# A first round of 432 rows for 448 in a three-layer kernel, and four instructions of the capacity at another place

## The chip, the core and the metric

The kernel runs on one core of one Trainium2 chip. The metric is the device time of one execution in microseconds (us). The core's engines run their own queues in order: TensorE (PE; PEld is its weight load), VectorE (DVE), ScalarE (ACT), GpSimd (POOL) and SyncE (SP, which issues most DMAs). Matmuls and extractions go through PSUM banks, everything else through SBUF.

## The reference

Three layers, one behind the other: a recurrent attention over 4 x 8 heads of 768 steps, a mixture of 8 experts with one expert a token, and a dense layer. Cut to the part that the change touches:

```
def _moe_ref(x, w_gate, w1, w2, capacity):
    logits = x @ w_gate                      # 3072 tokens, 320 numbers, 8 experts
    expert_idx = np.argmax(logits, axis=1)
    gate_w = softmax(logits)[arange(N), expert_idx]
    for i in range(N):                       # rows of an expert, in the order of tokens
        e = expert_idx[i]
        if counts[e] < capacity:             # capacity = N // E * 2 = 768
            disp[e, counts[e]] = x[i]; pos[i] = counts[e]; counts[e] += 1; keep[i] = True
    h = np.maximum(einsum('ecd,edf->ecf', disp, w1), 0.0)     # 320 -> 1024
    y = einsum('ecf,efd->ecd', h, w2)                         # 1024 -> 320
    out[i] = gate_w[i] * y[expert_idx[i], pos[i]] if keep[i] else 0

def _moe2_ref(x, w_in, w_out):               # 320 -> 2048 -> 320
    h = x @ w_in
    return np.where(h > 0, h, np.exp(np.minimum(h, 0)) - 1) @ w_out
```

All inputs are random; the router therefore spreads the 3072 tokens over the experts unevenly around 384.

## The kernel before

**Stages.** `attention` works through 24 units of 128 tokens, in an order that is written out by hand in the table `ORDER` (a word a step; `steps` maps the first letters to functions). `ffn` follows with the experts and the dense layer. While attention runs, TensorE, VectorE, ScalarE and GpSimd share its small steps; its last steps put the last units' rows in place.

**Rows of an expert.** `x_out` makes a unit's rows with their logits; `route` and `route_mm` give each row its number within its expert; `scatter` writes the rows with an indirect DMA from GpSimd (L567) into `disp`, a DRAM tensor in which expert e has ES rows and its first row is at e*ES + SL. The experts' *first round* takes SL rows of every expert as four tiles of SL/4. Rows behind a shorter expert's last are zero (`zero_d`). Expert 0's rows are read back by `first_rows` (step `F`, function `first`); the rows of the last two units don't make that trip, but are placed by a one-hot matmul (`hot`, L587 and L588 build it on VectorE).

**The expert stage.** `experts(0)` runs eight `Turned` blocks. A block's rows, transposed, stand in PSUM (`pt`); `prep` makes a high part XH (ScalarE, L953) and a low part XL (VectorE, L954: the transposed rows less XH). A block has eight steps f. `s1` of a step multiplies the weights with the rows: 8 matmuls with SL columns (L969: four with XH, two with XL, two with XS, which holds both parts of the last 64 numbers). ScalarE makes H (L1099), VectorE L (L1100), and three steps later `s2` multiplies H and L with the second weights: 8 matmuls with SL columns (L1034 to L1044). Four PSUM banks are shared by `s1` and the transposes. The next expert's rows come by DMA (L1086), are scaled by their gate (VectorE L1073 to L1079, ScalarE L1093) and are transposed on TensorE (L934) between the steps.

**Weights.** A half of an expert's weights (128 x 2816 numbers, 1408 KB) is fetched by SyncE into one of two buffers (L802, L804). `split` then makes a high part on ScalarE (L776, four a half) and a low part on GpSimd (L781, sixteen a half). A fetch waits until the split of the half two before it has read its buffer.

**Counts and the capacity.** `marks`, at the head of the expert stage, turns the 64-bit capacity into a float with four small VectorE instructions (L1262 to L1265) and sets constants on GpSimd (among them `one`, L1268). `counts`, during the first expert's steps, sums the experts' rows and derives the places of the outputs and the number of rounds: it is one if no expert has more rows than SL (or the capacity). `overflow` holds a loop for the later rounds; it makes the experts and the dense layer again.

**The dense layer.** Six blocks of 512 tokens take the experts' outputs in expert order from `xt` (L1303, L1304) and scatter the result to its tokens (L1314).

The lines at the head of the expert stage:

```
second = split(1)
go(second, 5)                     # half 1: four L776, sixteen L781
if not dyn:
    marks()                       # L1262 to L1275
bl[0].start(None if dyn else turned)      # L953, L954
fetch(2)
```

Of the kernel before, what the change touches and what calls it, by code (L numbers as in the profile page):

```python
# [20 lines left out]
D = 320  # L21
NTOK = 3072
SL = 448
ES = 8 * SL
# [51 lines left out]
def attention(tc, nc, e_in, v_tok, d_in, wg, disp, xt, cst, ring, early, early_w, cv, cap, after):  # L76
# [499 lines left out]
    def hot(u):  # L576

        xo, w = st["XO", u], slice(0, D + 1)
        if u < NU - 1:
# [8 lines left out]
        nc.vector.tensor_tensor(oh.rearrange("p (i r) -> p i r", i=4), cst["row"].unsqueeze(1).to_broadcast([128, 4, 112]),  # L588
                                p.unsqueeze(2).to_broadcast([128, 4, 112]), op=ALU.is_equal)
# [7 lines left out]
    def first():  # L597
        nc.gpsimd.iota(cst["row"], pattern=[[1, 112]], base=SL, channel_multiplier=0, allow_small_or_imprecise_dtypes=True)
        nc.gpsimd.iota(cst["off"], pattern=[[-112, 4]], base=0, channel_multiplier=0, allow_small_or_imprecise_dtypes=True)
        first_rows(nc, cst, disp)  # L600

    def zero_d(e):
        nc.sync.dma_start(out=disp[e * ES + SL:e * ES + 2 * SL, :].rearrange("(p i) d -> p (i d)", p=112).rearrange("p (x d) -> p x d", d=188),
                          in_=zr[0:112, 0:188].unsqueeze(1).to_broadcast([112, 7, 188]))

    def zero_x():
        nc.sync.dma_start(out=xt[D:D + 1, :].rearrange("o (p d) -> (o p) d", p=16), in_=zr[0:16])
# [58 lines left out]
    for i in range(4):  # L666
        for k, c in enumerate(cols):
            nc.tensor.matmul(turned[k][0:c.stop - c.start, 112 * i:112 * i + 112], X[0:112, i, c], ident[0:112, 0:112], start=False, stop=False)
# [7 lines left out]
def first_rows(nc, cst, disp):  # L676
    dv = disp.rearrange("(e r i p) d -> e r p i d", e=8, i=4, p=112)
    X = cst["x"][:, 0:4 * RW].rearrange("p (i d) -> p i d", i=4)
    for i in range(4):
        nc.sync.dma_start(out=X[0:112, i], in_=dv[0, 1][:, i])  # L680


def consts(p):
# [15 lines left out]
    c["row"] = c["x"][:, 1536 + RW:1648 + RW]  # L699
# [187 lines left out]
def ffn(tc, nc, cst, disp, xt, w1, w2, w32, out, ring, W0, cv, ps, turned):  # L887
# [19 lines left out]
    class Block:  # L907
# [91 lines left out]
        def out(s):  # L999
            s.Y = ap.tile([128, 1344], F32, tag="Y", name="Y")[:, 0:1280].rearrange("p (i d) -> p i d", i=4)  # L1000
# [16 lines left out]
    class Turned(Block):  # L1017
# [50 lines left out]
    def soft(s, tag="s", lg=None):  # L1068

        t = lambda nm, sh: ap.tile(sh, F32, tag=tag + nm, name=nm, bufs=1)[0:112]  # L1070
        g, x = t("g", [128, 4]), t("x", [128, 4, 8])
        lg = s.X[0:112, :, D + 1:RW] if lg is None else lg
        nc.vector.tensor_reduce(g, lg, axis=AX.X, op=ALU.max)  # L1073
        nc.vector.tensor_tensor(x, lg, g.unsqueeze(2).to_broadcast([112, 4, 8]), op=ALU.subtract)
# [7 lines left out]
    def rows(src, gate=True):  # L1082

        def load(s, now):
            s.X = s.XF[:, 0:4 * RW].rearrange("p (i d) -> p i d", i=4)
            nc.sync.dma_start(out=s.X[0:112], in_=src)  # L1086
# [5 lines left out]
            for i in range(4):  # L1092
                nc.scalar.mul(s.X[0:112, i, 0:D], s.X[0:112, i, 0:D], g[:, i:i + 1])  # L1093
# [22 lines left out]
    def gates():  # L1116
# [26 lines left out]
        nc.vector.scalar_tensor_tensor(out=t, in0=t, scalar=over["cap"], in1=OH, op0=ALU.is_lt, op1=ALU.mult)  # L1143
# [10 lines left out]
        nc.vector.scalar_tensor_tensor(out=epos, in0=eb, scalar=1.0 / 8, in1=pos, op0=ALU.mult, op1=ALU.add)  # L1154
# [30 lines left out]
    dv = disp.rearrange("(e r i p) d -> e r p i d", e=8, i=4, p=112)  # L1185
# [5 lines left out]
    def experts(r, dyn=False, more=None):  # L1191
# [4 lines left out]
        for e in range(8):  # L1196
            if dyn:
                src = dv[e, bass.ds(r, 1)].rearrange("r p i d -> (r p) i d")
                dst = yr[SL * e:SL * e + SL, :].rearrange("(i p) d -> p i d", p=112)

                def store(Y, i, dst=dst):
                    if i == 3:
                        nc.sync.dma_start(out=dst, in_=Y[0:112])
                bl.append(Block(Ws[e], rows(src), relu, store, P=112))
            else:
# [5 lines left out]
                bl.append(Turned(Ws[e], rows(dv[e, 1], e > 0), relu, store, P=112))  # L1211
# [47 lines left out]
    def marks():  # L1259

        cw, cf = cst["cap"], ap.tile([128, 4], F32, name="cf", bufs=1)
        nc.vector.tensor_copy(cf[:, 0:2], cw)  # L1262
        nc.vector.tensor_scalar(cf[:, 2:3], cf[:, 0:1], 0.0, 4294967296.0, op0=ALU.is_lt, op1=ALU.mult)
        nc.vector.scalar_tensor_tensor(out=cf[:, 3:4], in0=cf[:, 1:2], scalar=4294967296.0, in1=cf[:, 2:3], op0=ALU.mult, op1=ALU.add)
        nc.vector.tensor_tensor(cf[:, 3:4], cf[:, 3:4], cf[:, 0:1], op=ALU.add)  # L1265
        over["cap"] = cf[:, 3:4]
# [3 lines left out]
        for i in range(4):  # L1270
            nc.gpsimd.iota(start[:, i:i + 1], pattern=[[0, 1]], base=112 * i, channel_multiplier=1, allow_small_or_imprecise_dtypes=True)
# [5 lines left out]
    def late_gate(B):  # L1277

        yield
        lg = ap.tile([128, 4, 8], F32, name="lgx", bufs=1)[0:112]  # L1280
# [9 lines left out]
        for i in range(4):  # L1290
            nc.tensor.matmul(p[:, 112 * i:112 * i + 112], g[:, i:i + 1].to_broadcast([112, 128]), ident[0:112, 0:112], start=True, stop=True)
# [66 lines left out]
    def counts():  # L1358
# [14 lines left out]
        nc.vector.tensor_scalar(rn[:, 1:2], rn[:, 0:1], float(SL // 8), None, op0=ALU.add)  # L1373
        nc.vector.tensor_scalar(rn[:, 2:3], over["cap"], float(SL), None, op0=ALU.min)
# [8 lines left out]
        over["n"] = nc.values_load(ri[0:1, 0:1], min_val=1, max_val=8)  # L1383
# [122 lines left out]
```

## Time and profile before

| | us |
|---|---|
| three timed runs | 1041.87, 1044.39, 1047.43 (median 1044.39) |
| the profiled execution | 1040.54 |
| its span, first to last instruction | 1038.7 |
| TensorE busy | 950.6 (92%) |
| VectorE, GpSimd, ScalarE busy | 738.3, 617.1, 516.6 |
| mean granted TensorE clock | 0.952 |

The profiled execution is one run, 3.85 us under the median of the others. A busy time is a sum over the whole span; what a stage is bound by is read from that stage alone. Matmuls overlap in the records: one with 448 columns is shown with 0.36 us, but the next begins 0.20 us later, so that their pace is read from their starts. Starts are in us from the span's start.

### The profile page before, as it was taken

What the parts mean: (1) busy time and instruction counts of PE and PEld (TensorE: products, weight loads), DVE (VectorE), ACT (ScalarE), POOL (GpSimd) and SP (SyncE); (2) the same over time, 40 slices, a digit from 0 to 9 for tenths busy, and PEclk for the clock granted to TensorE, in tenths of its full rate; (3) what the DMA queues carried; (4) which work ended last, traced back from release to release, by engine and by line L of the source; (5) the groups of instructions that cost most, each with busy time, mean ns of one, the idle gap of its engine ahead of it and who ended that gap; (6) DMA issues with size and microseconds to landing.
All of it is one profiled execution on the core that took longest, in us unless ns stands there. A gap on an engine that the chain in (4) does not pass through costs nothing.

```text
span 1038.7 us, 25351 instructions
## 1 busy us (share of the span) xinstructions
PE 950.6 (92%) x9994; PEld 860.9 (83%) x9994; DVE 738.3 (71%) x1291; ACT 516.6 (50%) x1013; POOL 617.1 (59%) x929
## 2 busy tenths in 40 slices
PE   4758989989899999789999999999999999999993
PEld 4758878888789888678889888888899888899993
DVE  8846848788675687658778877576766777677760
ACT  3636635666454434245544555565555555554550
POOL 4766979489898833467768787953333333333332
PEclk9967889999899999989999999999999999999997
DMA  6758875666565774646776866501010000100000
GB/s 161 174 159 173 182 162 120 144 139 145 127 120 119 171 195 99 170 141 203 214 236 201 250 186 217 187 23 26 27 27 26 11 28 13 27 26 1 26 2 28
DMA packets 181448, 121.69 MB, mean 117 GB/s; under 512 B 106256, under 2 KB 167336, under 8 KB 179688
## 3 DMA queue, kind: packets, MB, share of 16 engines
q1 hardware_dynamic: 175652, 99.63, 38.0%
q10 hardware_dynamic: 2500, 9.21, 3.4%
q0 software_dynamic: 3168, 11.14, 3.0%
q8 instruction: 81, 1.33, 0.5%
q14 instruction: 47, 0.39, 0.1%
HBM read 86.89 MB, written 33.05 MB: 115 GB/s over the span
## 4 chain that ended last, share of the span: by engine, by line
PE 54%; DVE 17%; DMA 16%; issue 5%; ACT 3%; POOL 3%; SPq 0%; ACTq 0%; DVEq 0%; POOLq 0%
PE ph L969 20%; DMA ring<-in_e_in_dram 5%; PE po L995 5%; PE po L996 5%; PE po L997 5%; DMA w<-E 4%; PE q L482 2%; PE sc L234 2%; DVE L L1100 1%; DVE ring L200 1%; PE x L519 1%; DVE E L860 1%; PE ut L426 1%; PE y L509 1%; DMA dab<-AB 1%
## 5 line engine op out<-in xcount | busy, mean ns | idle before, releaser
L781 POOL TENSOR_TENSOR ring<-ring,ring 128x64 fp32r<-128x64 f32 (+2 forms) x320 | 204.7, 675 | 72.4 <-ACT ring L776 72.4
L1114 POOL TENSOR_TENSOR L<-E,H 128x512 fp32r<-128x512 f32 x66 | 91.6, 1388 | 169.2 <-ACT H L1113 152.5
L969 PE MATMUL ph<-XH,ring 128*128 128x512 f32 (+1 forms) x640 | 169.9, 387 | 0.8 <-ACT XH L953 0.8
L1107 ACT ACTIVATE E<-N 128x512 f32<-128x512 f32 x96 | 60.7, 632 | 152.8 <-DVE N L1106 78.9
L310 POOL TENSOR_TENSOR X<-X,ring 128x60 f32<-128x60 f32 (+19 forms) x170 | 120.4, 708 | 13.3
L969 PEld LDWEIGHTS ph<-XH,ring 128*128 128x128 f32 x640 | 115.7, 190 | 14.9 <-ACT XH L953 1.4
L997 PE MATMUL po<-ring,L 128*128 128x320 f32 x384 | 119.4, 311 | 1.6 <-POOL L L1114 1.6
L995 PE MATMUL po<-ring,H 128*128 128x320 f32 x384 | 119.4, 311 | 0.2 <-ACT H L1113 0.2
L996 PE MATMUL po<-ring,H 128*128 128x320 f32 x384 | 119.2, 310 | 0.0
L969 PE MATMUL ph<-XL,ring 128*128 128x512 f32 (+1 forms) x320 | 97.9, 387 | 7.5 <-DVE XL L954 7.5
L969 PE MATMUL ph<-XS,ring 128*128 128x512 f32 (+1 forms) x320 | 96.9, 384 | 0.0
L1111 DVE SCALAR_TENSOR_TENSOR M<-E,M 128x512 f32<-128x512 f32 x96 | 78.0, 812 | 16.1 <-ACT M L1108 16.1
L1106 DVE TENSOR_SCALAR N<-ph 128x512 f32<-128x512 f32 x96 | 65.8, 685 | 27.7 <-PE ph L969 27.4
L308 POOL TENSOR_TENSOR ring<-X,ring 128x60 f32<-128x60 f32 (+19 forms) x108 | 65.0, 602 | 34.4 <-DMA ring<-dab 26.3
L995 PEld LDWEIGHTS po<-ring,H 128*128 128x128 f32 x384 | 72.8, 190 | 5.2 <-ACT H L1113 0.5
L996 PEld LDWEIGHTS po<-ring,H 128*128 128x128 f32 x384 | 72.7, 189 | 4.0
L969 PEld LDWEIGHTS ph<-XL,ring 128*128 128x128 f32 x320 | 60.7, 190 | 18.4 <-DVE XL L954 8.2
L997 PEld LDWEIGHTS po<-ring,L 128*128 128x128 f32 x384 | 72.7, 189 | 2.1 <-POOL L L1114 2.1
L1112 DVE SCALAR_TENSOR_TENSOR E<-ph,M 128x512 f32<-128x512 f32 x96 | 66.4, 692 | 8.1 <-DVE M L1111 0.5
L969 PEld LDWEIGHTS ph<-XS,ring 128*128 128x128 f32 x320 | 60.3, 189 | 11.2 <-DVE XS L954 0.4
L1100 DVE SCALAR_TENSOR_TENSOR L<-ph,H 128x448 fp32r<-128x448 f32 x64 | 39.4, 616 | 41.3 <-ACT H L1099 41.2
L1113 ACT CAST H<-E 128x512 fp32r<-128x512 f32 x96 | 59.0, 614 | 13.5 <-DVE E L1112 10.4
(261 smaller groups left out, 2176.5 us busy)
## 6 DMA issues: line engine op xcount, KB each, us to landing
ring<-in_w_dram SPq DMA_DIRECT2D x16, 640.0 KB
ring<-in_w_dram SPq DMA_DIRECT2D x32, 256.0 KB
dab<-AB SPq DMA_DIRECT2D x24, 256.0 KB
ring<-in_e_in_dram ACTq DMA_DIRECT2D x18, 321.6 KB
ring<-w SPq DMA_DIRECT2D x4, 1408.0 KB
disp<-ring SPq DMA_DIRECT2D x8, 575.8 KB
S<-in_w_out_dram SPq DMA_DIRECT2D x13, 320.0 KB
ring<-in_w_dram SPq DMA_DIRECT2D x32, 128.0 KB
```

The lines of the kernel that those rows point to most:

```text
L308: nc.gpsimd.tensor_tensor(tv, X[:, 0:n, s:s + 1].to_broadcast([128, n, m]), N[:, s:s + 1, s + 1:e].to_broadcast([128, n, m]), op=ALU.mult)
L310: nc.gpsimd.tensor_tensor(X[:, 0:n, s + 1:e], X[:, 0:n, s + 1:e], tv, op=ALU.subtract)
L781: s.nc.gpsimd.tensor_tensor(B[:, to], r[:, q], B[:, q].bitcast(F32), op=ALU.subtract)
L969: nc.tensor.matmul(p, l, r[:, 0:s.T], start=i == 0, stop=i == len(seq) - 1)
L995: nc.tensor.matmul(o, H[:, c], hb, start=f == 0, stop=False)
L996: nc.tensor.matmul(o, H[:, c], lb, start=False, stop=False)
L997: nc.tensor.matmul(o, L[:, c], hb, start=False, stop=f == s.W.nf - 1)
L1106: nc.vector.tensor_scalar(N, p, 0.0, None, op0=ALU.min)
L1107: nc.scalar.activation(out=E, in_=N, func=AF.Exp)
L1111: nc.vector.scalar_tensor_tensor(out=M, in0=E, scalar=1.0, in1=M, op0=ALU.add, op1=ALU.mult)
L1112: nc.vector.scalar_tensor_tensor(out=E, in0=p, scalar=0.0, in1=M, op0=ALU.max, op1=ALU.add)
L1114: eng.tensor_tensor(L, E, H.bitcast(F32), op=ALU.subtract)
```

## The change

SL becomes 432, SR = SL // 4 = 108 is the height of a tile, and ES becomes 9 SL, so that nine rounds of 432 rows hold what eight of 448 did. What was written for 112 rows and for a factor of 8 is written with SR and ES / SL. The four instructions of the capacity move from `marks` to `first`, and their tile `cf` from a pool of the feed-forward part to the constants. Cut to its core:

```
-SL = 448
-ES = 8 * SL
+SL = 432
+SR = SL // 4
+ES = 9 * SL
@@ hot
-oh "p (i r)": cst["row"] ... [128, 4, 112], p ... [128, 4, 112], op=ALU.is_equal
+oh "p (i r)": cst["row"] ... [128, 4, SR], p ... [128, 4, SR], op=ALU.is_equal
@@ first (step F)
+        cw, cf = cst["cap"], cst["cf"]
+        nc.vector.tensor_copy(cf[:, 0:2], cw)
+        nc.vector.tensor_scalar(cf[:, 2:3], cf[:, 0:1], 0.0, 4294967296.0, op0=ALU.is_lt, op1=ALU.mult)
+        nc.vector.scalar_tensor_tensor(out=cf[:, 3:4], in0=cf[:, 1:2], scalar=4294967296.0, in1=cf[:, 2:3], op0=ALU.mult, op1=ALU.add)
+        nc.vector.tensor_tensor(cf[:, 3:4], cf[:, 3:4], cf[:, 0:1], op=ALU.add)
-        nc.gpsimd.iota(cst["row"], pattern=[[1, 112]], base=SL, ...)
-        nc.gpsimd.iota(cst["off"], pattern=[[-112, 4]], base=0, ...)
+        nc.gpsimd.iota(cst["row"], pattern=[[1, SR]], base=SL, ...)
+        nc.gpsimd.iota(cst["off"], pattern=[[-SR, 4]], base=0, ...)
         first_rows(nc, cst, disp)
@@ consts
-    c["cap"] = p.tile([128, 2], I32, name="CAP")
+    c["cap"], c["cf"] = p.tile([128, 2], I32, name="CAP"), p.tile([128, 4], F32, name="CF")
@@ marks
-        cw, cf = cst["cap"], ap.tile([128, 4], F32, name="cf", bufs=1)
-        nc.vector.tensor_copy(cf[:, 0:2], cw)
-        ... the other three
-        over["cap"] = cf[:, 3:4]
         one = over["one"] = ap.tile([128, 8], F32, name="one", bufs=1)
@@ experts
-                bl.append(Turned(Ws[e], rows(dv[e, 1], e > 0), relu, store, P=112))
+                bl.append(Turned(Ws[e], rows(dv[e, 1], e > 0), relu, store, P=SR))
@@ counts
-        nc.vector.tensor_scalar(rn[:, 1:2], rn[:, 0:1], float(SL // 8), None, op0=ALU.add)
+        nc.vector.tensor_scalar(rn[:, 1:2], rn[:, 0:1], ES / SL, float(SL), op0=ALU.mult, op1=ALU.add)
-        nc.vector.tensor_scalar(rg, cst["ebase"], 1.0 / 8, rn[:, 1:2], op0=ALU.mult, op1=ALU.is_lt)
+        nc.vector.tensor_scalar(rg, cst["ebase"], 1.0, rn[:, 1:2], op0=ALU.mult, op1=ALU.is_lt)
-        over["n"] = nc.values_load(ri[0:1, 0:1], min_val=1, max_val=8)
+        over["n"] = nc.values_load(ri[0:1, 0:1], min_val=1, max_val=9)
```

In the loop of later rounds the division by 8 becomes one by 9, which takes one more instruction; the run shown doesn't enter that loop.

The order of instructions differs on VectorE alone; on the other engines the same instructions stand in the same order with smaller shapes. VectorE at the head of the expert stage, before (the one-hot of the last unit, the capacity, the low parts of the first expert's rows, two steps' L, and the second expert's row scaling):

```order
L588 TENSOR_TENSOR hot<-X_73,pos 128x448
L1262 CAST cf<-CAP 128x2
L1263 TENSOR_SCALAR cf<-cf 128x1
L1264 SCALAR_TENSOR_TENSOR cf<-cf 128x1
L1265 TENSOR_TENSOR cf<-cf 128x1
L954 TENSOR_TENSOR XL<-pt,XH 128x448 x2
L954 TENSOR_TENSOR XS<-pt,XS 64x448
L1100 SCALAR_TENSOR_TENSOR L<-ph,H 128x448 x2
```

The same place after the change:

```order
L589 TENSOR_TENSOR hot<-X_74,pos 128x432
L960 TENSOR_TENSOR XL<-pt,XH 128x432 x2
L960 TENSOR_TENSOR XS<-pt,XS 64x432
L1106 SCALAR_TENSOR_TENSOR L<-ph,H 128x432 x2
L1079 TENSOR_REDUCE g<-X_74 108x4
L1080 TENSOR_TENSOR x<-X_74,g 108x32
L1365 COPY cnt<-pc 128x8
L1367 SCALAR_TENSOR_TENSOR cs<-one,cnt 128x8
L1368 CAST bi<-cs 128x8
```

The low parts follow the one-hot with nothing between them; the scan and the CAST of the counts stand behind the second expert's logits as before. VectorE some 11 us earlier, at the step `F` after the change (the routing of unit 22, then the mask multiplication of the last unit's scores, which its y matmul reads); before, L547 was followed by L487 at once:

```order
L545 TENSOR_TENSOR roh<-req,rm_6292 128x8
L548 TENSOR_TENSOR ACC<-ACC,roh 128x8
L600 CAST CF<-CAP 128x2
L601 TENSOR_SCALAR CF<-CF 128x1
L602 SCALAR_TENSOR_TENSOR CF<-CF 128x1
L603 TENSOR_TENSOR CF<-CF 128x1
L488 TENSOR_TENSOR Qs<-q,mask 128x512 x2
```

The four stand there between the routing and the mask multiplication.

## Rows read from the trace of the kernel before

**Rows 1.** Stages: start:end and length, busy us (instructions) of five engines, clock, DMA.

```profile
437.40:665.50 228.10, 217.46 (x1094) 194.25 (x1095) 174.79 (x314) 116.11 (x215) 176.47 (x281) 0.98 0.66 201
665.50:1017.00 351.50, 349.69 (x1912) 312.97 (x1911) 246.18 (x352) 182.09 (x321) 131.33 (x137) 1.00 0.08 25
```

**Rows 2.** Timeline, expert stage's head: start, length, engine, line, tiles, count, [idle before].

```profile
436.72 8.28 POOL L781 TENSOR_TENSOR ring<-ring,ring 128x64 fp32r<-128x64 f32 x16
436.83 0.97 ACT L953 CAST XH<-pt 128x448 fp32r<-128x448 f32 x2 [2.56 <-PE pt L593]
436.85 8.24 DVE L1262 CAST cf<-CAP 128x2 f32<-128x2 int32 x1 [2.60 <-DMA ring<-in_w_dram]
437.41 1.30 PE L969 MATMUL ph<-XH,ring 128*128 128x448 f32 x4 [0.75 <-ACT XH L953]
...
445.58 1.15 DVE L954 TENSOR_TENSOR XL<-pt,XH 128x448 fp32r<-128x448 f32 x2
446.25 1.27 PE L969 MATMUL ph<-XL,ring 128*128 128x448 f32 x2 [7.54 <-DVE XL L954]
446.76 0.62 DVE L954 TENSOR_TENSOR XS<-pt,XS 64x448 fp32r<-64x448 f32 x1
...
450.87 1.06 PE L969 MATMUL ph<-XH,ring 128*128 128x448 f32 x4
```

**Rows 3.** One microsecond of that hole, columns as in rows 1.

```profile
440.00:441.00 1.00, 0.00 (x0) 0.00 (x0) 1.00 (x1) 0.00 (x0) 1.00 (x3) 0.50 0.24 32
```

**Rows 4.** Timeline of TensorE: one step with 448 columns, then the output stage.

```profile
655.86 0.96 PE L969 MATMUL ph<-XH,ring 128*128 128x448 f32 x4
...
659.06 0.96 PE L969 MATMUL ph<-XH,ring 128*128 128x448 f32 x4
...
759.82 0.30 PE L995 MATMUL po<-ring,H 128*128 128x320 f32 x1
...
761.57 1.09 PE L969 MATMUL ph<-XH,ring 128*128 128x512 f32 x4
762.51 0.63 PE L969 MATMUL ph<-XL,ring 128*128 128x512 f32 x2
```

**Rows 5.** Groups of TensorE by form: count, busy us, mean ns, idle before.

```profile
L969 PE MATMUL ph<-XH,ring 128*128 128x448 f32 x256 | 64.9, 375 | 0.8 <-ACT XH L953 0.8
L1042 PE MATMUL po<-L,ring 128*64 128x448 f32 x64 | 23.3, 365 | 0.0
L934 PE MATMUL pt<-ident,X 112*128 112x112 f32 x56 | 11.8, 280 | 3.1 <-ACT X L1093 0.7
```

**Rows 6.** The fetch of half 3, the DMA behind it, its first cast; columns as above.

```profile
445.03 2.22 SPq L802 DMA_DIRECT2D ring<-in_w_dram  x4
...
445.00:451.50 6.50, 5.25 (x16) 4.08 (x17) 2.87 (x8) 1.54 (x3) 0.49 (x8) 0.60 0.76 215
...
460.06 0.78 ACT L776 CAST ring<-ring 128x704 fp32r<-128x704 f32 x1
```

**Rows 7.** Timeline at the place to which the four instructions go.

```profile
424.47 1.52 DVE L544 TENSOR_TENSOR roh<-req,rm 128x8 bf16<-128x8 f32 x1
...
425.09 0.87 POOL L584 TENSOR_TENSOR hot<-XO,hot 128x321 fp32r<-128x321 f32 x1
...
426.11 1.28 DVE L487 TENSOR_TENSOR Qs<-q,mask 128x512 f32<-128x512 f32 x2
...
426.84 1.28 PE L509 MATMUL y<-Qs,KB 128*64 128x64 f32 x32
```

**Rows 8.** Small VectorE instructions beside L781, and all low parts (min/median/max ns).

```profile
406.22 1.73 DVE L527 COPY XO<-LG 128x9 f32<-128x9 f32 x1
...
455.43 0.35 DVE L1078 TENSOR_SCALAR g<-g 112x4 f32<-112x4 f32 x1
...
L954 DVE TENSOR_TENSOR XL<-pt,XH x16: 607/616/625, 445.6 to 633.8; 128x448 fp32r<-128x448 f32 x16
```

**Rows 9.** Timeline: row scaling of a later expert, and the matmul behind it.

```profile
514.68 1.92 ACT L1093 ACTIVATE X<-X,g 112x320 f32<-112x320 f32 x4 [1.45 <-DVE g L1079]
...
516.74 1.06 PE L969 MATMUL ph<-XH,ring 128*128 128x448 f32 x4
```

More of the change, by code (lines that the diff above doesn't have):

```diff
@@ L667, in attention @@
         for k, c in enumerate(cols):
-            nc.tensor.matmul(turned[k][0:c.stop - c.start, 112 * i:112 * i + 112], X[0:112, i, c], ident[0:112, 0:112], start=False, stop=False)
+            nc.tensor.matmul(turned[k][0:c.stop - c.start, SR * i:SR * i + SR], X[0:SR, i, c], ident[0:SR, 0:SR], start=False, stop=False)
     do(f"D{NU-1}", f"H{NU-1}")
@@ L999, in out @@
         def out(s):
-            s.Y = ap.tile([128, 1344], F32, tag="Y", name="Y")[:, 0:1280].rearrange("p (i d) -> p i d", i=4)
+            s.Y = ap.tile([128, 3 * SL], F32, tag="Y", name="Y")[:, 0:1280].rearrange("p (i d) -> p i d", i=4)
         def evict(s, i):
@@ L1068, in soft @@
     def soft(s, tag="s", lg=None):
[L1070 removed]
+        t = lambda nm, sh: ap.tile(sh, F32, tag=tag + nm, name=nm, bufs=1)[0:SR]
         g, x = t("g", [128, 4]), t("x", [128, 4, 8])
[L1072 removed]
+        lg = s.X[0:SR, :, D + 1:RW] if lg is None else lg
         nc.vector.tensor_reduce(g, lg, axis=AX.X, op=ALU.max)
[L1074 removed]
+        nc.vector.tensor_tensor(x, lg, g.unsqueeze(2).to_broadcast([SR, 4, 8]), op=ALU.subtract)
         nc.scalar.activation(out=x, in_=x, func=AF.Exp)
@@ L1085, in load @@
             s.X = s.XF[:, 0:4 * RW].rearrange("p (i d) -> p i d", i=4)
-            nc.sync.dma_start(out=s.X[0:112], in_=src)
+            nc.sync.dma_start(out=s.X[0:SR], in_=src)
             yield
@@ L1142, in gates @@
                                 b.unsqueeze(3).to_broadcast([128, 2, 8, 12]), op=ALU.add)
-        nc.vector.scalar_tensor_tensor(out=t, in0=t, scalar=over["cap"], in1=OH, op0=ALU.is_lt, op1=ALU.mult)
+        nc.vector.scalar_tensor_tensor(out=t, in0=t, scalar=cst["cf"][:, 3:4], in1=OH, op0=ALU.is_lt, op1=ALU.mult)
         kp = T("kp", [128, 24])
@@ L1198, in experts @@
                 src = dv[e, bass.ds(r, 1)].rearrange("r p i d -> (r p) i d")
-                dst = yr[SL * e:SL * e + SL, :].rearrange("(i p) d -> p i d", p=112)
+                dst = yr[SL * e:SL * e + SL, :].rearrange("(i p) d -> p i d", p=SR)
                 def store(Y, i, dst=dst):
                     if i == 3:
-                        nc.sync.dma_start(out=dst, in_=Y[0:112])
-                bl.append(Block(Ws[e], rows(src), relu, store, P=112))
+                        nc.sync.dma_start(out=dst, in_=Y[0:SR])
+                bl.append(Block(Ws[e], rows(src), relu, store, P=SR))
             else:
@@ L1279, in late_gate @@
         yield
-        lg = ap.tile([128, 4, 8], F32, name="lgx", bufs=1)[0:112]
+        lg = ap.tile([128, 4, 8], F32, name="lgx", bufs=1)[0:SR]
         with nc.allow_non_contiguous_dma("the logits of a row"):
@@ L1290, in late_gate @@
         for i in range(4):
-            nc.tensor.matmul(p[:, 112 * i:112 * i + 112], g[:, i:i + 1].to_broadcast([112, 128]), ident[0:112, 0:112], start=True, stop=True)
+            nc.tensor.matmul(p[:, SR * i:SR * i + SR], g[:, i:i + 1].to_broadcast([SR, 128]), ident[0:SR, 0:SR], start=True, stop=True)
         yield
```

36 lines of the change are left out of this document (17 added, 19 removed).

## The prediction

> **What bounds the kernel now.** I read the stage table first, then the stretch between attention and experts in order of time. From 437.4 us TensorE has work in nearly every microsecond: 217.46 of the 228.10 us of the expert stage, 349.69 of the 351.50 us of the output stage [rows 1]. So a shorter matmul is paid back in time there, and so is any hole in TensorE. The largest hole is at the head of the expert stage [rows 2]: ScalarE has the first high part XH at about 437.35 and TensorE begins, but VectorE, which must make the low part XL, sits in the capacity's CAST (L1262, two numbers a row) for 8.24 us, from 436.85 to 445.09. GpSimd's run of 16 weight subtractions (L781) lies from 436.72 to 445.00. VectorE goes on within 0.1 us of its end; TensorE waited 7.54 us for XL and restarts at 446.25. In the hole the granted clock fell to 0.50, its 1.2 GHz level [rows 3], and the mean from 445 to 451.5 was still 0.60 [rows 6].
>
> **The change, part by part.** All sums are made against the profiled execution, 1040.54 us (span 1038.7); the median of the three timed runs, 1044.39, lies 3.85 us above it, and I shift the result by that.
>
> *A. The four instructions leave the head of the stage.* Without them XL can start at 437.4. Three extractions of 0.6 us (1.15 us for two, 0.62 for the third [rows 2]) end at about 439.1 instead of 447.38. The two last matmuls of step f=0 take 0.4 us, the eight of f=1 take 1.6 us, the count's small one 0.1, so f=2 begins at 441.2 instead of 450.87 [rows 2]: 9.7 us, of which some 1.5 us is the slow clock that the hole had brought. Bounds: 8.2 us (the wait alone) to 10.5 us. What the extraction meets is GpSimd's same run; 16 such extractions lie in this stage, most beside L781, with a maximum of 625 ns against a median of 616 [rows 8], so I take it as not held.
>
> *B. What is late next.* Two things stay where they were, because they hang on GpSimd's end at 445.0. (i) VectorE's scan of the counts (L1366) reads the tile `one`, which GpSimd sets after its run; behind it on VectorE are the low part of f=2 and the row scaling of the second expert, and then ScalarE's four multiplications (1.92 us in the like place [rows 9]); the second expert's first transposes come perhaps 0.9 us late. (ii) The fetch of weight half 3 is issued at 445.03, when the run frees its buffer. By 451.5 the DMA has moved 6.5 us x 215 GB/s = 1.40 MB, which is one half (1408 KB); ScalarE first casts it at 460.06 [rows 6]. Moved 9.7 us forward that is 450.4, so ScalarE waits 1 to 2 us. TensorE runs three steps ahead of ScalarE's output and feels a part, say 0.7. Together +1.6; from 0 (all covered) to +4.5 (a wait that the four PSUM banks don't cover).
>
> *C. 432 columns for 448.* A step has eight matmuls in s1 and eight in s2. From 655.86 to 659.06 sixteen matmuls of 448 columns take 3.20 us, 200 ns each; twelve of 320 take 1.75 us, 146 ns each; four of 512 take 0.94 us, 235 ns each [rows 4]. Below 448 a column costs 54/128 = 0.42 ns, above it 35/64 = 0.55 ns. Sixteen columns are 6.7 ns, at most 8.8. There are 64 steps (64 of each s2 line, 256 of s1's four on XH [rows 5]), so 64 x 16 = 1024 matmuls; 1024 x 6.7 = -6.9 us, at most -9.0. I take the first, since 432 lies on that side. The transposes lose 4 of 112 columns: 4/112 of 11.8 us [rows 5] is 0.4 at most; I count -0.3.
>
> *D. A wait that grows.* From the third expert on TensorE waits for the scaled rows: ScalarE scales from 514.68 to 516.60, and the matmul behind the transposes starts only at 516.74 [rows 9]. That chain hangs on the end of the expert before and hardly shrinks, while the two steps of TensorE beside it end 32 x 6.7 ns = 0.2 us sooner. I take +0.15 in six experts, +0.9 (0 to +1.5).
>
> *E. The four instructions at their new place.* They stand behind L547 and ahead of the mask multiplication L487, which the last y matmul (426.84) waits for [rows 7]; from there the chain goes on to the last rows. From the CAST's end, 445.09, to XL at 445.58 the other three take 0.49 us; with 0.16 for a CAST that is not held that is +0.65. GpSimd is idle there after L584 ends at 425.96. If it is not, the CAST can be held until that end: +1.0. Nothing shortens there, so no gain.
>
> *At nothing:* the zero stores, 756 pieces for 784, are issued early in attention and read at its end; ES = 9 SL only moves addresses; the extractions and stores of 432 columns are 17 ns shorter on engines that are not the bound; the output stage keeps 512 columns.
>
> Sum: -9.7 + 1.6 - 6.9 - 0.3 + 0.9 + 0.65 = -13.75 us. 1040.54 - 13.75 = 1026.8, and for the median 1044.39 - 13.75 = **1030.6 us**.
>
> **The rivals.**
>
> *1. The hold is inherited by XL.* What held the CAST is not proved to be its form; a copy of nine numbers (L527) was once held 1.73 us, over three subtractions, while L1078, also on four numbers a row, got in after 0.35 us [rows 8]. If the first VectorE instruction at this place is held whatever it is, XL starts at 445.0, A is 0.6 and B is 0: -0.6 - 6.9 - 0.3 + 0.9 + 0.65 = -6.25, 1038.1 us. For it: nothing else in the trace was held for 16 instructions. Against: the extractions' maximum of 625 ns. The Trainium skill, "SBUF — State Buffer", section "Who interferes with whom", says that a cast and a GpSimd instruction exclude each other and that the loser is blocked until the first instruction finishes. By that rule one subtraction, at most 0.65 us, would be the CAST's price and the other 7.6 us something else, which could stay; the row of 8.24 us over 16 subtractions does not agree with it. 0.10.
>
> *2. The next cast is held.* After the scan at 445.1 comes L1367, a CAST of the counts, beside the next run of subtractions; two of the four casts that feed it are then done, so eight subtractions, 4.2 us at the run's 0.52 us each [rows 2]. The row scaling hangs behind it, and TensorE stands still for some 4.3 us more: 1034.9 us. L1078's 0.35 us speaks against it [rows 8]. 0.13.
>
> *3. The expert stage does not follow the shorter matmuls.* VectorE is busy 174.79 and GpSimd 176.47 of 228.10 us [rows 1], 77% each; if their work in order sets the pace, C and D are zero: 1037.2 us. TensorE's near-full row speaks against it. 0.08.
>
> *4. Slower: a second round runs.* Where an expert has more than 432 rows, the loop that handles later rounds is entered, which the run before did not need: all experts and the whole output stage once more, 228.10 + 351.50 us [rows 1] and the loop's own gathers, over 1610 us. It decides at 433 rows. The reference's own routing of its inputs gives 421, 323, 414, 388, 357, 423, 371 and 375 rows, 423 at most. 0.02.
>
> **How the numbers follow.** Forecast 0.65, rivals 0.10, 0.13, 0.08, 0.02, the rest (0.02) unnamed. The forecast's own range, from the ends of A to E, is about -17.5 to -9, 1027 to 1035.5; the three runs shown spread over 5.6 us, so the median may lie 3 us off. 1024 to 1038 takes in rivals 2 and 3 and leaves out 4 and half of 1. A measurement tells about 0.5%, 5.2 us, from no change: the forecast and rivals 2 and 3 lie clearly beyond it, rival 1 just at it. Faster: 0.65 + 0.13 + 0.08 + half of rival 1, less something for the runs' spread, 0.88; same 0.09, slower 0.03.
>
> **What would show it.** In the changed profile: the four instructions at about 426.2, under 0.2 us each, and the y matmul 0.65 us later; XL within 0.1 us of XH, not held; TensorE without the 7.5 us wait and the clock at 1.00 from 437 on; step f=2 at about 442; 193 ns from matmul to matmul; ScalarE's first cast of half 3 waiting for a DMA; the output stage starting some 14 us earlier and lasting as long as before. It is wrong if XL or L1367 shows a duration of microseconds, if the step stays 3.2 us, or if the loop's instructions appear.

## The result, and the profile after

The changed kernel takes 1035.84 us (median of 12 runs, 1028.33 to 1039.29) for 1044.34 before (12 runs): the ratio is 0.9902, 95% interval 0.9874 to 0.9931, so 10.2 us less (7.2 to 13.2); the medians by themselves lie 8.5 apart. 13.75 were forecast. The profiled execution has a span of 1034.7 us.

The stages of after, columns as in [rows 1], cut where TensorE begins the experts' first matmul and the output stage's first:

```profile
442.86:660.53 217.67, 212.29 (x1094) 194.13 (x1094) 163.62 (x309) 113.10 (x213) 175.80 (x280) 0.99 0.68 210
660.53:1012.00 351.47, 348.25 (x1908) 312.32 (x1906) 236.79 (x352) 181.53 (x323) 137.13 (x139) 1.00 0.08 25
```

Cut in the same way, the expert stage of before lasts 228.05 us (437.41 to 665.46), so it became 10.4 us shorter; the rest of the program behind it goes from 373.2 to 374.2. The stage begins 5.45 us later than in before. The change does not account for that: the four traces with 432 columns and the four instructions in attention (this one and e3, e5 and e10 below) begin it between 438.93 and 443.09, and e2, which leaves the move out, at 442.13. From here on I compare the expert stage.

Its head in after (timeline: start, length, engine, line, tiles, count, idle before):

```profile
442.16 8.41 POOL L787 TENSOR_TENSOR ring<-ring,ring 128x64 fp32r<-128x64 f32 x16
442.29 0.94 ACT L959 CAST XH<-pt 128x432 fp32r<-128x432 f32 x2 [2.48 <-PE pt L594]
442.84 1.12 DVE L960 TENSOR_TENSOR XL<-pt,XH 128x432 fp32r<-128x432 f32 x2 [3.06 <-DMA ring<-in_w_dram]
442.86 1.27 PE L975 MATMUL ph<-XH,ring 128*128 128x432 f32 x4 [0.74 <-ACT XH L959]
...
446.76 1.03 PE L975 MATMUL ph<-XH,ring 128*128 128x432 f32 x4
```

The low part starts as soon as the first high part is made (442.84), and two of its instructions take 1.12 us, beside GpSimd's run of 16. The third step begins 3.90 us behind the first; it was 13.46 in [rows 2]. The four instructions stand in attention and are short:

```profile
430.90 0.17 DVE L548 TENSOR_TENSOR ACC<-ACC,roh 128x8 bf16<-128x8 bf16 x1
...
430.99 0.17 DVE L600 CAST CF<-CAP 128x2 f32<-128x2 int32 x1
...
431.57 0.16 DVE L603 TENSOR_TENSOR CF<-CF 128x1 f32<-128x1 f32 x1
431.64 1.28 DVE L488 TENSOR_TENSOR Qs<-q,mask 128x512 f32<-128x512 f32 x2
```

One step, to be held against [rows 4], and the third expert's row scaling with the transposes that wait for it, to be held against [rows 9]:

```profile
657.42 0.94 PE L975 MATMUL ph<-XH,ring 128*128 128x432 f32 x4
...
660.53 1.09 PE L975 MATMUL ph<-XH,ring 128*128 128x512 f32 x4
```

```profile
483.36 1.92 ACT L1099 ACTIVATE X<-X,g 108x320 f32<-108x320 f32 x4 [1.45 <-DVE g L1085]
483.98 1.80 PE L940 MATMUL pt<-ident,X 108*128 108x108 f32 x4 [1.12 <-ACT X L1099]
485.46 1.79 PE L975 MATMUL ph<-XH,ring 128*128 128x432 f32 x4
```

A step takes 3.11 us for 3.20. But TensorE now stands before the transposes (idle 1.12 us), and the four matmuls behind them take 1.79 us for 0.94: the mean granted clock is 0.91 in the 20 us from 482.86 on, for 1.00 in the 40 us before.

For the comparisons I worked three numbers out of every trace: the stage as cut above; the **pitch**, the mean distance from start to start of two matmuls of the experts without a wait between them (about 930 to 950 a trace); and the **block**, a fifth of the time from the third expert's first transpose to the eighth's.

| kernel | columns | stage us | pitch ns | block us |
|---|---|---|---|---|
| before | 448 | 228.05 | 200.5 | 28.28 |
| after | 432 | 217.67 | 195.1 | 27.98 |
| e1_move_only | 448 | 220.63 | 203.5 | 28.38 |
| e2_size_only | 432 | 217.44 | 195.3 | 27.78 |
| e3_rows_early | 432 | 216.38 | 195.2 | 28.08 |
| e5_ring_back | 432 | 222.17 | 195.0 | 28.93 |
| e6_size_old_tile | 432 | 227.78 | 196.2 | 28.29 |
| e7_two_inputs | 432 | 224.76 | 196.3 | 27.69 |
| e8_two_runs | 432 | 222.36 | 196.1 | 28.08 |
| e9_behind_low | 432 | 221.19 | 196.2 | 27.82 |
| e10_less_432 | 432 | 216.35 | 195.1 | 26.85 |
| e11_less_448 | 448 | 216.71 | 203.6 | 27.71 |
| e12_both_aligned | 448 | 221.03 | 203.5 | 28.49 |

Each row is one execution. after, e2 and e5 do the same work in this stage behind its head and differ by 4.7 us in the stage and by 1.15 in the block, so one stage bears no conclusion on a few us, and one block none on some tenths; timed ratios and repeated readings do. The pitch repeats within 0.3 ns. e7, e8, e9 and e12 are one execution each and have no timed ratio; e4 stands in its own section.

### The profile page after: what moved, and what is told of

It reads as the page before. It is cut to its first block, busy times and chain, and to the rows that moved or that the text cites. A ratio compares the mean times of both kernels' runs of the same rounds, so it can differ in the third digit from the quotient of the medians.

```text
span 1034.7 us, 25350 instructions
## 1 busy us (share of the span) xinstructions
PE 952.0 (92%) x9994; PEld 867.5 (84%) x9994; DVE 717.6 (69%) x1291; ACT 512.5 (50%) x1013; POOL 620.6 (60%) x929
## 4 chain that ended last, share of the span: by engine, by line
PE 43%; DVE 15%; POOL 13%; issue 11%; DMA 10%; ACT 3%; SPq 3%; ACTq 0%; POOLq 0%; DVEq 0%
PE ph L975 14%; POOL L L1120 4%; POOL ring L309 4%; PE q L483 3%; PE po L1001 3%; PE po L1002 3%; PE po L1003 3%; POOL X L311 3%; DMA w<-E 2%; DMA dab<-AB 2%; PE x L520 2%; PE ut L427 1%; DMA ring<-in_e_in_dram 1%; DVE L L1106 1%; PE sc L235 1%
## 5 line engine op out<-in xcount | busy, mean ns | idle before, releaser
L1120 POOL TENSOR_TENSOR L<-E,H 128x512 fp32r<-128x512 f32 x66 | 96.9, 1467 | 164.1 <-ACT H L1119 149.0
L975 PE MATMUL ph<-XH,ring 128*128 128x512 f32 (+1 forms) x640 | 167.5, 383 | 0.7 <-ACT XH L959 0.7
L975 PEld LDWEIGHTS ph<-XH,ring 128*128 128x128 f32 x640 | 115.6, 189 | 13.3 <-ACT XH L959 1.4
L311 POOL TENSOR_TENSOR X<-X,ring 128x60 f32<-128x60 f32 (+19 forms) x170 | 114.7, 675 | 13.3
L975 PE MATMUL ph<-XL,ring 128*128 128x512 f32 (+1 forms) x320 | 96.7, 384 | 0.0
L975 PE MATMUL ph<-XS,ring 128*128 128x512 f32 (+1 forms) x320 | 95.8, 380 | 0.1
L309 POOL TENSOR_TENSOR ring<-X,ring 128x60 f32<-128x60 f32 (+19 forms) x108 | 70.6, 654 | 35.2 <-DMA ring<-dab 17.9
L1117 DVE SCALAR_TENSOR_TENSOR M<-E,M 128x512 f32<-128x512 f32 x96 | 68.9, 717 | 20.7 <-ACT M L1114 20.7
L975 PEld LDWEIGHTS ph<-XS,ring 128*128 128x128 f32 x320 | 60.7, 190 | 10.4 <-DVE XS L960 0.4
L975 PEld LDWEIGHTS ph<-XL,ring 128*128 128x128 f32 x320 | 60.4, 189 | 9.0
L1106 DVE SCALAR_TENSOR_TENSOR L<-ph,H 128x432 fp32r<-128x432 f32 x64 | 38.4, 601 | 40.6 <-ACT H L1105 40.5
L782 ACT CAST ring<-ring 128x704 fp32r<-128x704 f32 x80 | 61.1, 778 | 7.5 <-DMA ring<-w 5.4
```

Of the source, the lines that this page charges most:

```text
L309: nc.gpsimd.tensor_tensor(tv, X[:, 0:n, s:s + 1].to_broadcast([128, n, m]), N[:, s:s + 1, s + 1:e].to_broadcast([128, n, m]), op=ALU.mult)
L311: nc.gpsimd.tensor_tensor(X[:, 0:n, s + 1:e], X[:, 0:n, s + 1:e], tv, op=ALU.subtract)
L782: s.nc.scalar.copy(B[:, 0:704], r)
L975: nc.tensor.matmul(p, l, r[:, 0:s.T], start=i == 0, stop=i == len(seq) - 1)
L1117: nc.vector.scalar_tensor_tensor(out=M, in0=E, scalar=1.0, in1=M, op0=ALU.add, op1=ALU.mult)
L1120: eng.tensor_tensor(L, E, H.bitcast(F32), op=ALU.subtract)
```

## Experiments: one part at a time

**e1_move_only.** Before, with the move alone.

```
 SL = 448
+        (in first) the four instructions, on cst["cf"]
-        (in marks) the four instructions
```

> The kernel before with 448 columns; only the four capacity instructions go to step F. Read by the expert stage, from TensorE's first s1 matmul to the output stage's first (228.05 us before, 217.67 after). Theory: the head of the stage gives back 9.5 us (8.2 of VectorE's hold and the slow clock behind it), and 1 to 1.5 of that is lost again where the third expert's transposes wait for the row scaling, because VectorE has won only the 8.2: stage 219.5 to 220.5, time about 8 us under before. Rival: whatever stands first on VectorE there inherits the hold; then XL lasts about 8 us, and the stage stays within 1 us of 228. Second rival: nothing is lost at the third expert, stage 218.5.

Ratio 0.9921 (0.9881 to 0.9961), 8.2 us less; stage 220.63 us, 7.4 less. The head behaves as in after: third step 4.0 us behind the first, no hold on the low part (0.62 us each). The rival of an inherited hold falls. Of the 9.4 us won at the head, two are missing at the stage's end, but not where the theory put them: the third expert's transposes wait only 0.2 us more than the step before them needs. The pitch rose instead, from 200.5 to 203.5 ns: 1024 x 3 ns = 3.1 us, which more than covers them. (That is taken up in the section on the pitch.)

**e2_size_only.** After, with the four instructions back in `marks`; their tile stays among the constants.

> The kernel after with 432 columns, the four instructions back at the head of the expert stage (their tile stays with the constants). Theory: the CAST is held again until GpSimd's sixteen subtractions end, 8.2 us, wherever its tile lies, and of the shorter matmuls (195 ns for 201, 1024 of them, 5.6 us) about half is lost in the waits for the row scaling: stage 225 to 226 us. Rival: the shorter matmuls count in full, stage 222 to 223. Second rival: the CAST was held through the pool that its tile came from (the list of releases that its first user waits for); then it takes 0.2 us here and the stage is near 218.

Ratio 0.9895 (0.9823 to 0.9967), stage 217.44: as fast as after, against the theory. The second rival holds. VectorE in e2:

```profile
438.44 0.61 DVE L589 TENSOR_TENSOR hot<-X,pos 128x432 fp32r<-128x432 f32 x1
438.96 0.16 DVE L1264 CAST CF<-CAP 128x2 f32<-128x2 int32 x1
...
442.11 1.12 DVE L955 TENSOR_TENSOR XL<-pt,XH 128x432 fp32r<-128x432 f32 x2 [2.41 <-ACT XH L954]
```

The CAST follows the one-hot at once, 3.2 us ahead of the stage and of GpSimd's run (442.15), in a gap in which VectorE waits anyway. In [rows 2] VectorE stood idle for 2.60 us before the same CAST; the profile puts that down to a DMA on a weight buffer. There the CAST is the first user of a pool that takes over memory from attention's tiles. Which of their releases it waits for is not shown; that the pool brings the wait is (the next run). The wait put it beside the run.

**e6_size_old_tile.** The same with the tile in its old pool: only the size is changed.

```
-        cw, cf = cst["cap"], cst["cf"]
+        cw, cf = cst["cap"], ap.tile([128, 4], F32, name="cf", bufs=1)
```

> Only the size is changed: 432 columns, the four instructions at the head of the expert stage and their tile from the feed-forward part's pool, as before. (In e2_size_only the tile stayed with the constants, the CAST waited for nothing, ran 3 us ahead of the stage in 0.16 us, and nothing was lost.) Theory: as first user of its pool the CAST waits for the DMAs of the buffers that lay there, so it starts only when GpSimd's sixteen subtractions have begun, and is held to their end: duration 8 to 8.5 us, third step 13 us behind the first for 3.9, stage 223 to 226 us. Rival: with the stage some microseconds later the pool is free in time, CAST 0.2 us, stage near 217. The ring of weights is at 0 in 64 here: pitch as in e5_ring_back.

Ratio 0.9997 (0.9964 to 1.0029), stage 227.78: nothing is left of the gain. VectorE and GpSimd:

```profile
438.21 0.17 DVE L1264 CAST cf<-CAP 128x2 f32<-128x2 int32 x1 [3.16 <-DMA ring<-in_w_dram]
438.42 0.16 DVE L1265 TENSOR_SCALAR cf<-cf 128x1 f32<-128x1 f32 x1
438.61 8.10 DVE L1266 SCALAR_TENSOR_TENSOR cf<-cf 128x1 f32<-128x1 f32 x1
...
439.00 8.29 POOL L782 TENSOR_TENSOR ring<-ring,ring 128x64 fp32r<-128x64 f32 x16
```

The wait is back (3.16 us) and so is the hold, this time on the third of the four: one number a row, 8.10 us. Against e2, which differs in the tile's pool alone (and so in the addresses behind it, 1 ns a matmul), the third step comes 9.8 us later. And with the hold in place as in before, 432 columns for 448 gave between 3.8 us less and 3.0 more in the time, where the pitches (196.2 ns for 200.5) would allow 4.4 us less. The stage became 0.3 us shorter here and 3.3 in e7, which is held as long: single stages do not settle it.

## Experiments: what holds VectorE

**e7_two_inputs.** e6 with the CAST as an instruction with two inputs.

```
-        nc.vector.tensor_copy(cf[:, 0:2], cw)
+        nc.vector.tensor_tensor(cf[:, 0:2], cw, cw, op=ALU.max)
```

> e6_size_old_tile with the CAST written as the maximum of the capacity's words with themselves, an instruction with two inputs (int32 in, float out, the same numbers). Theory: it is the form with one SBUF input and no second that is held to the end of GpSimd's run; two inputs get in after at most one subtraction, 0.2 to 0.7 us, and the stage is near 217. Rival: whatever starts beside the run with all operands in SBUF is held to its end, 8 us again.

```profile
436.17 7.92 DVE L1264 TENSOR_TENSOR cf<-CAP 128x2 f32<-128x2 int32 x1 [2.54 <-DMA ring<-in_w_dram]
...
436.39 8.28 POOL L782 TENSOR_TENSOR ring<-ring,ring 128x64 fp32r<-128x64 f32 x16
```

Held for 7.92 us, stage 224.76: the theory of the one-input form falls.

**e8_two_runs.** e6 with GpSimd's constants between the eighth and the ninth subtraction.

```
-        go(second, 5)
+        go(second, 2)
         marks()
+        go(second, 3)
```

> e6_size_old_tile with GpSimd's constants (memsets and iotas) placed between the eighth and the ninth of the sixteen subtractions; all other orders stay. Theory: the CAST is held as long as GpSimd's subtractions follow one another without a gap; the first break frees it, so 4.2 us, third step about 9 us behind the first, stage some 4 us shorter than e6_size_old_tile. Rival: the hold ends only when GpSimd has nothing queued or at a fixed point, 8.5 us or more.

```profile
440.70 4.19 DVE L1265 CAST cf<-CAP 128x2 f32<-128x2 int32 x1 [2.53 <-DMA ring<-in_w_dram]
...
441.26 4.17 POOL L782 TENSOR_TENSOR ring<-ring,ring 128x64 fp32r<-128x64 f32 x8
445.38 0.09 POOL L1271 MEMSET one<- 128x8 f32 x1
```

4.19 us beside a run of eight that takes 4.17; the third step 9.38 us behind the first, the stage 5.4 us shorter than in e6. The hold ends 0.54 us ahead of the run's end, in e6 and e7 0.58: a run half as long holds half as long.

**e9_behind_low.** e6 with the four instructions behind the low parts.

```
         marks()                                    # without the four
         bl[0].start(None if dyn else turned)       # L954, L955
+        nc.vector.tensor_copy(cf[:, 0:2], cw)
+        ... the other three
```

> e6_size_old_tile with the four capacity instructions behind the three low parts of the first expert's rows, in the middle of GpSimd's run of sixteen subtractions for at its beginning. The long holds seen so far (before, e6, e7, e8 and two shorter ones in attention) all began while GpSimd ran an indirect DMA or within 0.2 us of the first subtraction behind one. Theory: only there does the hold reach to the end of the run; in the middle each of the four waits for one subtraction at most, 0.15 to 0.7 us, and the third step begins 4 to 5 us behind the first, stage 217 to 219 us. Rival: any VectorE instruction with all operands in SBUF is held to the end of the run; then the CAST lasts 5 to 6 us, VectorE's L of the first steps comes late, and the third step begins 8 us or more behind the first.

```profile
440.07 8.36 POOL L782 TENSOR_TENSOR ring<-ring,ring 128x64 fp32r<-128x64 f32 x16
...
440.96 0.60 DVE L955 TENSOR_TENSOR XS<-pt,XS 64x432 fp32r<-64x432 f32 x1
441.59 6.96 DVE L1237 CAST cf<-CAP 128x2 f32<-128x2 int32 x1
```

The last low part, which reads PSUM, takes 0.60 us inside the run; the CAST right behind it is held to the run's end (448.55 against 448.43). So it is not the beginning of the run that matters, nor the indirect DMA ahead of it, during which the holds of e6, e7 and e8 began: the theory falls again. The rival has the hold right and its effect wrong: the third step is in time here (3.89 us), and the loss comes at the second expert's transposes, 17.8 us behind the stage's begin for 11.8 in after (stage 221.19).

What these traces, before and e10 (below) show together: an instruction of VectorE whose inputs all lie in SBUF can be held to within 0.6 us of the end of a run of GpSimd subtractions, whatever its form; the low parts from PSUM never were (0.63 us at most, 24 in each of the 14 traces). Not settled is why others get through: in e1 to e9 VectorE's conversions from SBUF (L865 to L877 in after) run beside such subtractions with 0.5 us or less added to their shortest durations; the addition L874 was slowed by up to 1.2 (in attention), the output stage's L1117 by up to 2.8.

## Experiments: what sets the pace of a block

**e3_rows_early.** After, with gate and scaling of the next expert's rows one step earlier from the third expert on.

```
-            yield
+            if not early:
+                yield
             g = yield from soft(s)
             ... four nc.scalar.mul
             yield
+            if early:
+                yield
```

> The kernel after, where from the third expert on the gate and the scaling of the next expert's rows are made one step earlier, the transposes in the same step as before: one step of TensorE lies between them. Theory: the waits ahead of and between these transposes, and the slow clock behind the third expert's, vanish: they are 9 us in the stage, less up to 3 where VectorE is late for something else: stage 209 to 212 us, 6 to 9 us under after. Rival: VectorE, GpSimd and the DMA set the pace of a block; then the wait moves to the weights' casts or to the low parts, stage within 2 us of 217.7.

Ratio 0.9897 (0.9826 to 0.9967), stage 216.38: the rival. TensorE's waits behind the first 15 us, after and e3 (waited for, us in total, times, longest):

```profile
PE pt L940 <- ACT X L1099: 2.6, 5, 1.1
```

```profile
PE ph L975 <- DVE L L1109: 4.7, 6, 1.3
PE po L1045 <- DVE Y L1054: 1.7, 3, 1.0
```

The waits for the scaled rows are gone, and nothing is won. In their place TensorE waits for PSUM banks that VectorE has not yet read: low parts (L) in the same step, evictions (Y) in the step before.

**e10_less_432** and **e11_less_448.** After and e1, with six of seven VectorE instructions of each weight conversion left out in the expert stage.

```
+            if end == 28:
+                v.tensor_scalar(A, hi, 3, 0x3FFFFFFF, op0=ALU.logical_shift_left, op1=ALU.bitwise_and)
+                ... stores and yields as before
+            else:
                 ... the seven instructions
```

> The kernel after with six of the seven VectorE instructions of every piece of the dense layer's weight conversion left out in the expert stage (its DMAs and one instruction stay; the dense layer then works with wrong weights). That takes some 85 of VectorE's 165 us out of the stage. Theory (in blocks 2 to 7 VectorE, in order, is late with row scaling and evictions, and so takes back what shorter matmuls save): TensorE's waits behind the first 15 us fall from 11.6 us to under 5, stage 209 to 212 us for 217.67. Rival: GpSimd's subtractions (184 of 218 us busy) and the weights' DMA set the pace: stage within 2 us of 217.7.

> e1_move_only (448 columns, the four instructions moved) with the same left out of VectorE. Theory: without VectorE in the way the matmuls count in full: e10_less_432 lies below this one by 1024 x (203.5 - 195.1 ns) = 8.6 us in the stage, where after lies below e1_move_only by 3.0. This stage: 217 to 220 us for 220.63. Rival: with VectorE relieved the two still differ by 3 us or less, so something else holds the pace.

The stages are 216.35 and 216.71, the ratios 0.9892 (0.9851 to 0.9933) and 0.9851 (0.9779 to 0.9924): the theory's 8.6 us between the two are not there, and taken as a whole e11's rival came true. The stage of e10, columns as in [rows 1]:

```profile
438.93:655.28 216.35, 210.72 (x1093) 194.33 (x1094) 92.50 (x178) 114.59 (x215) 148.50 (x284) 0.99 0.73 221
```

VectorE's busy time fell to 92.50 us (163.62 in after), but GpSimd's fell with it, to 148.50 (175.80), since its subtractions of 128x213 take 661 ns each for 772. So the two engines were relieved together.

The blocks say more. They take 26.85 us at 432 columns and 27.71 at 448, each less than every loaded trace with the same columns in the table (27.69 to 28.93 and 28.28 to 28.49): the load on the two engines costs a block some time. Relieved, the two lie 0.86 apart of the 128 x 8.5 ns = 1.09 that the pitches allow; loaded, the means of the seven traces at 432 (after, e2, e5 to e9) and of the three at 448 are 28.08 and 28.38, 0.30 apart, where the mean pitches allow 0.87. That points to VectorE, working in order, as what keeps back more than half of what shorter matmuls give. It is not shown: the 0.86 rests on one trace each, and GpSimd is not told apart from VectorE. And e10's last block loses what the others won:

```profile
624.49 21.17 POOL L787 TENSOR_TENSOR ring<-ring,ring 128x64 fp32r<-128x64 f32 x40 [2.67 <-ACT ring L782]
...
636.05 10.14 DVE L1079 TENSOR_TENSOR XL<-X,XH 128x512 fp32r<-128x512 f32 x1
...
646.77 0.46 PE L1054 MATMUL po<-L,ring 128*128 128x432 f32 x1 [3.60 <-DVE L L1114]
```

It is the hold once more. The output stage's first low part reads SBUF, not PSUM. It starts inside GpSimd's run of 40 subtractions (624.49 to 645.65), 18 of which begin behind it, and ends 0.54 us behind the run; TensorE waits 3.60 us, and the mean granted clock is 0.65 from 646 to 650. In after the same instruction also lies inside a run (56 subtractions, 635.62 to 668.92) and passes:

```profile
646.76 0.89 DVE L1071 TENSOR_TENSOR XL<-X,XH 128x512 fp32r<-128x512 f32 x1
```

So no run here tells what decides between a hold to the run's end and a passage within a microsecond.

## Experiments: what sets the pitch

**e4_sl424.** After with 424 columns (tiles of 106; two buffers keep their size).

```
-SL = 432
+SL = 424
-XC = NTOK + SL
+XC = NTOK + 432
-    s.Y = ap.tile([128, 3 * SL], F32, ...)
+    s.Y = ap.tile([128, 1296], F32, ...)
```

> The kernel after with 424 columns in tiles of 106. If the pitch follows the columns it falls by 8 x 0.42 = 3.4 ns from 195 to about 192; if the spread of 189 to 203 ns seen with 432 columns means a floor, it stays at 193 or above. Theory on the stage: since from the third expert on the row scaling sets when the transposes come, only about half of 1024 x 3.4 ns = 3.5 us shows, stage 215.5 to 217. Rival: all of it shows, stage near 214.

The pitch is 193.6, between the two expectations. The kernel is far slower, which neither theory nor rival had: ratio 1.1255 (1.1173 to 1.1337), stage 266.56. The transfers whose outer dimension is 106 rows are slow: from first to last packet the 424 rows of an expert take 12.9 to 14.0 us, where 448 take 2.5 to 4.5 and 432 take 2.8 to 4.7. The waits of the expert stage in e4:

```profile
PEld pt L940 <- ACT X L1099: 49.4, 28, 7.4
DVE g L1079 <- DMA X<-disp: 44.4, 7, 9.2
```

The zero stores, issued in attention, hold the queue in the same way: the expert stage begins at 541.19. In the packet records of such a transfer 2.1 packets are in flight on average, against 6 to 13.5 in before and after. The Trainium skill, "DMA: Bandwidth & Descriptors", section "Why a DMA increments its semaphore by 16 and not by 1", says that a transfer uses the largest number of engines up to 16 that divides the outer dimension of both its sides; that is 16 for 112 rows, 12 for 108 and 2 for 106, and the 2.1 packets in flight agree for the last. Between 112 and 108 no run here shows a loss.

**e5_ring_back.** After with the capacity's tile 64 bytes a row.

```
-    ... p.tile([128, 4], F32, name="CF")
+    ... p.tile([128, 16], F32, name="CF")
```

> The kernel after, its capacity tile 16 numbers a row wide for 4 (64 bytes for 16). In after that tile among the constants moved the ring of weights from an address that is 0 in 64 bytes to one that is 32 in 64; with 448 columns and this move alone the pitch of the matmuls rose from 200.5 to 203.5 ns (before against e1_move_only), 512 columns fell from 234.0 to 232.5. Here the ring is at 0 again. Theory (the address sets the pitch): 432 columns 192 to 194 ns for 195.1, 512 columns 234.0 again, 320 columns 146.8 for 146.2; 1024 matmuls at 1.3 to 3 ns less are 1.3 to 3 us, of which the row scaling takes some back: stage 215.5 to 217 for 217.67. Rival (something else in the removal of the hole): 195.1 stays, 512 stays at 232.5.

**e12_both_aligned.** e1 with the same edit.

> e1_move_only with the capacity's tile 64 bytes wide, which puts the ring of weights and the moving rows both at 0 in 64 bytes. So far: ring 0 and rows 32 (before) 200.5 ns at 448 columns and 234.0 at 512; ring 32 and rows 32 (e1_move_only) 203.5 and 232.5; ring 0 and rows 0 (e5_ring_back) 195.0 at 432 and 232.5 at 512, as with 32 and 32. Theory: it is the distance of the two addresses in 64 bytes that sets the pitch: 203.5 ns at 448 and 232.5 at 512 here. Rival: the ring's own address sets it: 200.5.

e5 went the rival's way: 195.0 ns, and 512 columns stay at 232.5 (ratio 0.9929, 0.9892 to 0.9966; stage 222.17). In e5 the rows of L975 (XH, XL, XS) had moved to 0 in 64 bytes along with the ring, which I had not taken into account. e12 then put the two theories against each other, and the distance won: 203.5 ns at 448 columns and 232.5 at 512, as with both at 32. (The addresses are those at which the built programs place the tiles.) All readings by this distance, ns:

| addresses in 64 bytes | 424 | 432 | 448 | 512 |
|---|---|---|---|---|
| equal (after, e1 to e5, e10 to e12) | 193.6 | 195.0 to 195.3 | 203.5 to 203.6 | 232.3 to 232.6 |
| 32 apart (before, e6 to e9) | | 196.1 to 196.3 | 200.5 | 233.3 to 234.0 |

At 448 columns, 32 apart, there is one trace, before; weights at 32 with rows at 0 no run has. e9 is 32 apart without the hole in TensorE at the head, so the hole is not what sets the pitch. One step of e12 and of e6: 3.25 us and 3.17 us.

```profile
649.11 0.97 PE L974 MATMUL ph<-XH,ring 128*128 128x448 f32 x4
652.36 0.97 PE L974 MATMUL ph<-XH,ring 128*128 128x448 f32 x4
```

```profile
660.20 0.96 PE L970 MATMUL ph<-XH,ring 128*128 128x432 f32 x4
663.37 0.96 PE L970 MATMUL ph<-XH,ring 128*128 128x432 f32 x4
```

## Why the prediction was right, and where it was not

The direction, the main cause and the range held; the gain was put 3.5 us too high by the ratio and 5.2 by the medians (1035.84 for 1030.6). The fault lies in step C and in the low chance of rival 3. The range held because it was drawn wide enough for rivals 2 and 3. The forecast's own, 1027 to 1035.5, would have missed the median by 0.3 us, though the ends of A to E, added up, reach from -19.2 to -8.4, that is from 1025.2 to 1036.0.

*A, -9.7.* The head won 9.56 us (third step 3.90 behind the first, for 13.46), with the clock at 1.00 in the first 40 us. Right in size. The reason given for the low part was incomplete: it reads PSUM, and no low part from PSUM was held in any trace (0.60 us inside e9's run). Rival 1 was wrong about XL, but right that the CAST's form is not the cause: other forms with all inputs in SBUF were held as well (e6, e7). What I missed altogether is that the hold needed the wait for the pool ahead of it; with the tile among the constants no move was needed (e2).

*B, +1.6.* Neither of its two mechanisms brought a loss: VectorE's scan did wait for `one` (0.56 us), but the second expert's transposes did not come late, and ScalarE did not wait for half 3. What came instead, the third expert's transposes waiting 1.3 us for the row scaling and a slow clock behind them, stands in after, e2 and e5, where the head is won and the columns are 432; with the move alone (e1) it is 0.2 us. e1 as a whole gave -7.4 in the stage and -8.2 timed, where A and B make -8.1: that is luck, for the 2.0 us that e1 lost behind its head are covered by the risen pitch (3.1 us).

*C, -6.9.* This is the step that failed. First in its price: the pitch fell by 5.4 ns, not 6.7, so 1024 matmuls give 5.5 us. The line through 320 and 448 columns does not hold, because the pitch also hangs on two addresses, and the moved tile changed their distance. Second, and more, in counting the matmuls in full: behind the head the stage of after won 0.8 us, and with the hold left as it was (e6) 432 columns gave nothing measurable in time. In the five blocks that the table compares, before and after differ by 0.30 us a block for 0.69 of matmul time. Where the rest stays is shown in part: waits that are taken away at one place come back where TensorE meets VectorE at another (e3), and the load on VectorE and GpSimd lengthens the blocks (e10, e11). Which of the two engines sets the limit is open.

*D, +0.9.* The mechanism was right, its size and its kind too small: the row scaling is one of several places at which TensorE meets VectorE's order. TensorE's time beyond the pitch, behind the first 15 us, rose from 7.4 to 11.6 us; the same sum is 8 to 17 us in the other traces at 432 columns (e2, e5 to e9) and 6 to 7 in e1 and e12 at 448.

*E, +0.65.* From the end of L548 to L488 lie 0.57 us, at a 0.17 us CAST. As forecast on VectorE; what the path lost by it can't be read, since the stage's begin spreads over 4 us.

*At nothing.* The zero stores: right for 108 rows; e4 shows that it was not safe to say so from the number of pieces alone. The output stage kept its 512 columns, but their pitch fell from 234.0 to 232.5 ns with the moved tile; its time did not fall with it in this pair (373.2 to 374.2).

*Rival 2* (the next CAST is held) did not come: L1368 took 0.20 us, between two runs. *Rival 3* (C and D zero) had 0.08, and the median lies nearer to it than to the forecast. (Its own terms, with the transposes' 0.3 at zero too, make -7.45 and 1036.9, not 1037.2.) I set against it that TensorE's busy row is nearly full; that row hides it, since the lost time lies in many gaps of 0.25 to 1.3 us. *Rival 4* did not come.

With the measured terms: 9.56 us at the head; behind it the stage won 0.8 more, 5.5 us of shorter matmuls less 4.7 that came back. That is 10.4 in the stage; less 0.6 for E and 1.0 behind the stage it is 8.8, where the ratio gives 10.2 (7.2 to 13.2).

The Trainium skill, "SBUF — State Buffer", section "Who interferes with whom", says that a VectorE instruction with two SBUF inputs, or one such as a cast in a mode that uses both pairs of ports, contends with GpSimd, and that whichever issues first has the shared pair for the whole instruction while the other is blocked. The instructions held here are of kinds that it names, and the low parts from PSUM, with one SBUF input, passed, as it has it. How long does not agree: the third instruction of e6 was held for 8.10 us, over a run of 16, and e10's low part for 10.14, while the conversions' 0.5 us or less is about one subtraction.

## What to carry to other kernels

A small VectorE instruction on SBUF data beside a long back-to-back run of GpSimd can cost all that is left of the run: look for small instructions with a duration of microseconds, and ask first which wait put them there. Before a smaller tile is credited with its matmul time, do the size alone with everything else as it was. And a tile that moves between pools moves every address behind it.

## What the runs showed of the hardware that I had not expected

- A held VectorE instruction ends within 0.6 us of the end of GpSimd's run: 8.24, 8.10, 7.92 and 6.96 us beside sixteen subtractions, 4.19 beside eight, 10.14 inside the last part of 40. It struck a cast, a two-input instruction on one number a row and a subtraction of 128x512 alike; other instructions passed beside such runs, and what decides is open.
- The pitch of these matmuls is not a line in the columns: with equal addresses in 64 bytes 8 columns from 424 to 432 cost 1.5 ns and 16 from 432 to 448 cost 8.4. Weights and rows 32 bytes apart make 448 columns 3.0 ns faster (one trace), 432 about 1 ns slower and 512 0.8 to 1.5 ns slower.
- 106 rows for 108 make the load of an expert's rows three to four times as long on average (13 us for 2.8 to 4.7).
